# The second MLP's first layer by seven products of halves in place of eight, with its gates split in the last layer

## The chip, the cores and the metric

The kernel runs on one core of a Trainium2 chip. The metric is the time of one execution in microseconds (us) on the device. The engines are named as the profile names them: PE (TensorE matmul), PEld (its weight load), DVE (VectorE), ACT (ScalarE), POOL (GpSimd) and SP (the engine that issues the transfers). Matrices lie in SBUF with 128 partitions; matmul results go to PSUM, which has eight banks of 512 float32 columns.

## The reference

A causal attention feeds two MLPs in a row; all inputs are float32.

```python
attn_out = _attn_ref(q, k, v)                 # 2 batches x 12 heads x 448 x 64, causal softmax
x = attn_out.transpose(0, 2, 1, 3).reshape(896, 768)

def _moe_ref(x, w_gate, w_val, w_out):        # 768 -> 1536 -> 768
    g = x @ w_gate
    silu = g * (1.0 / (1.0 + np.exp(-g)))
    val = x @ w_val
    return silu * val @ w_out

def _moe2_ref(x, w_in, w_out):                # 768 -> 2048 -> 768
    h = x @ w_in
    relu6 = np.clip(h + 3.0, 0.0, 6.0)
    g = h * relu6 / 6.0
    return g @ w_out
```

## The kernel before

**Products in three.** The weights arrive as 64-bit floats. Each MLP product is made from two float32r parts of each operand, a high part (the operand rounded) and a low part (the rest): `mm3_parts` (L183) issues high x high, high x low and low x high into one PSUM bank. So each term of a product is three matmuls of a 128 x 128 weight tile with 384 or 512 token columns (`PARTS`; 896 tokens together).

**Weights.** `w_unit` makes one unit of 768 x 128 weights (or 256 x 384 in the last layer): a DMA to `raw`, an unpacking on ACT (L112), a shift and an OR on DVE (L117, L118; the OR reads `raw` and `w`, both in SBUF), the high part on ACT (`whi`, L121), the low part on POOL (`wlo`, L122; it reads `w` and `whi`). The units run in a ring of four `whi`/`wlo` slots, three `raw` and two `w` buffers, two units ahead of their use; the cast to a slot waits until PE has done the slot's old unit. Each engine works through its own queue in order.

**Stages.** Attention comes first. The gate and value layers of the first MLP follow (24 units, 864 matmuls, results to `g1`), then w_out (12 units, 432 matmuls, results to `x2`), then the second MLP's first layer (16 units, one per block f of 128 hidden features, 576 matmuls), then the last layer in two column halves (L566, 672 matmuls of 384 columns: the gates are the weight tiles, the weights the moving operand). For a block f, both token parts are gated: a clipped ramp on ACT (L554), its product with the result on DVE (L555), then `split` makes the gates' high part on ACT (L165) and their low part on DVE (L166). The last layer reads these parts in both column halves.

**Order.** A scheduler merges the code into one queue for each engine; `high_priority` (`SOON`) puts the work on results ahead. The last layer keeps its last two weight units (`LATE`) for an end in which the token tiles finish one after the other.

## Time and profile before

| | |
|---|---|
| median of 3 runs | 616.59 us (616.4 to 617.06) |
| profiled execution | 616.48 us, span 614.7 us |
| PE busy | 608.2 us (99%), 3617 matmuls |
| DVE, ACT, POOL busy | 280.5, 265.4, 183.4 us |
| DMA | 70.15 MB, mean 114 GB/s |

Start with the share of PE and the chain that ended last. The mean duration of a matmul is longer than the distance between two, because they overlap; distances are read from the timeline. The means of ACT, DVE and POOL are durations of one instruction from its start to its end; two independent ones behind each other overlap by some 0.09 us.

### The profile page before, as it was taken

Reading aid. Unit: us, or ns where it says so; the run is one execution under the profiler, and the core shown is the slowest. Engines: PE = TensorE matmul, PEld = TensorE weight load, DVE = VectorE, ACT = ScalarE, POOL = GpSimd, SP = SyncE. Lnnn points to the kernel's source line nnn. Section 1 sums busy time; section 2 is a strip of 40 time slices with the busy share of each in tenths; the row PEclk is TensorE's granted clock in tenths of the full one; section 3 lists DMA queues with packets and bytes.
Section 4 is the critical chain, followed back from the end, with each engine's and each line's share of the span. In section 5 each row is a group of like instructions: output and inputs, shape, how many; then the busy total and the mean of one; then the engine's idle time right before and its main releaser. Section 6 shows DMA issues by size and latency. Waiting matters only on the chain.

```text
span 614.7 us, 9332 instructions
## 1 busy us (share of the span) xinstructions
PE 608.2 (99%) x3617; PEld 561.9 (91%) x3618; DVE 280.5 (46%) x622; ACT 265.4 (43%) x452; POOL 183.4 (30%) x126
## 2 busy tenths in 40 slices
PE   8999999999999999999999999999999999999997
PEld 5999999889999888889999888889998899999997
DVE  6888888675433344334322333454544542123001
ACT  5687777745433333333323223555545532223100
POOL 4555653233222222222222222222222222213200
PEclk9999999999999999999999999999999999999999
DMA  9555545356433333333333333333433333452002
GB/s 181 133 131 128 137 113 157 111 189 213 151 107 104 103 102 103 103 114 124 121 104 102 103 103 102 104 109 115 129 110 103 102 103 103 107 177 65 0 1 91
DMA packets 83917, 70.15 MB, mean 114 GB/s; under 512 B 35232, under 2 KB 79776, under 8 KB 83872
## 3 DMA queue, kind: packets, MB, share of 16 engines
q1 hardware_dynamic: 83872, 69.55, 39.2%
q8 instruction: 29, 0.48, 0.3%
q14 instruction: 16, 0.13, 0.1%
HBM read 61.73 MB, written 2.75 MB: 105 GB/s over the span
## 4 chain that ended last, share of the span: by engine, by line
PE 97%; DVE 1%; ACT 1%; issue 0%; POOL 0%; DVEq 0%; ACTq 0%
PE mm L183 61%; PE mm L566 19%; PE pv L414 6%; PE sc L343 5%; PE tp L386 4%; PE tr L268 1%; PE zero L207 1%; PE tr L448 1%; DVE e L356 0%; DVE qq L281 0%; PE tr L298 0%; POOL wlo L122 0%; ACT e L366 0%; ACT w L112 0%; DVE qq L314 0%
## 5 line engine op out<-in xcount | busy, mean ns | idle before, releaser
L122 POOL TENSOR_TENSOR wlo<-w,whi 128x768 fp32r<-128x768 f32 (+1 forms) x69 | 126.1, 1828 | 356.7 <-ACT whi L121 299.7
L117 DVE TENSOR_SCALAR w<-w 128x768 uint32<-128x768 uint32 (+1 forms) x69 | 39.9, 578 | 191.1 <-ACT w L112 191.0
L121 ACT CAST whi<-w 128x768 fp32r<-128x768 f32 (+1 forms) x69 | 57.0, 826 | 127.7 <-PE mm L183 85.4
L183 PE MATMUL mm<-x1h,wlo 128*128 128x384 f32 (+1 forms) x288 | 105.0, 365 | 0.4 <-POOL wlo L122 0.4
L183 PE MATMUL mm<-x1l,whi 128*128 128x384 f32 (+1 forms) x288 | 104.7, 364 | 0.0
L183 PE MATMUL mm<-x1h,whi 128*128 128x384 f32 (+1 forms) x288 | 104.6, 363 | 0.0
L112 ACT ACTIVATE w<-raw 128x768 f32<-128x768 f32 (+1 forms) x69 | 61.1, 887 | 95.8 <-POOL wlo L122 95.3
L566 PE MATMUL mm<-whi,gl 128*128 128x384 f32 x224 | 74.8, 334 | 0.0
L566 PE MATMUL mm<-whi,gh 128*128 128x384 f32 x224 | 74.8, 334 | 0.0
L566 PE MATMUL mm<-wlo,gh 128*128 128x384 f32 x224 | 74.8, 334 | 0.0
L414 PE MATMUL pv<-v,et 112*112 112x65 f32 x480 | 73.4, 242 | 0.0
L183 PE MATMUL mm<-x2h,wlo 128*128 128x384 f32 (+1 forms) x192 | 69.9, 364 | 0.0
L118 DVE SCALAR_TENSOR_TENSOR w<-raw,w 128x768 uint32<-128x768 uint32 (+1 forms) x69 | 69.1, 1002 | 1.7
L183 PE MATMUL mm<-x2l,whi 128*128 128x384 f32 (+1 forms) x192 | 69.8, 364 | 0.0
L183 PE MATMUL mm<-x2h,whi 128*128 128x384 f32 (+1 forms) x192 | 69.6, 362 | 0.0
L414 PEld LDWEIGHTS pv<-v,et 112*112 112x112 f32 x480 | 65.6, 177 | 1.2
L386 PE MATMUL tp<-ident,e 112*112 112x112 f32 x240 | 61.2, 260 | 1.2 <-ACT e L366 1.2
L183 PEld LDWEIGHTS mm<-x1h,whi 128*128 128x128 f32 x288 | 54.1, 188 | 6.4 <-ACT whi L121 0.4
L183 PEld LDWEIGHTS mm<-x1h,wlo 128*128 128x128 f32 x288 | 54.0, 188 | 6.3 <-POOL wlo L122 0.6
L183 PEld LDWEIGHTS mm<-x1l,whi 128*128 128x128 f32 x288 | 54.1, 188 | 6.1
L366 ACT ACTIVATE e<-e,m 112x336 f32<-112x336 f32 (+1 forms) x96 | 48.7, 530 | 19.9 <-DVE m L356 19.9
L165 ACT CAST gh<-mm 128x384 fp32r<-128x384 f32 (+1 forms) x56 | 29.6, 529 | 53.3 <-DVE mm L520 26.4
(71 smaller groups left out, 1019.5 us busy)
## 6 DMA issues: line engine op xcount, KB each, us to landing
raw<-in_moe_w_out_dram SPq DMA_DIRECT2D x28, 768.0 KB, 4.3
raw<-in_moe_w_in_dram SPq DMA_DIRECT2D x16, 768.0 KB, 4.6
raw<-in_moe_w_gate_dram SPq DMA_DIRECT2D x12, 768.0 KB, 4.2
raw<-in_moe_w_val_dram SPq DMA_DIRECT2D x12, 768.0 KB, 4.3
kn<-in_k_dram SPq DMA_DIRECT2D x24, 112.0 KB, 2.7
qn<-in_q_dram SPq DMA_DIRECT2D x24, 112.0 KB, 2.7
v<-in_v_dram SPq DMA_DIRECT2D x12, 224.0 KB, 3.2
out_dram<-ob SPq DMA_DIRECT2D x14, 192.0 KB, 1.8
```

The source lines that it names most:

```text
L112: first = nc.scalar.activation(out=w[:, p], in_=high.bitcast(F32), func=AF.Prelu, scale=2.0**-112, alpha=2.0**32)
L117: nc.vector.tensor_scalar(out=wu, in0=wu, scalar1=3, scalar2=None, op0=ALU.logical_shift_left)
L118: nc.vector.scalar_tensor_tensor(out=wu, in0=low, scalar=29, in1=wu, op0=ALU.logical_shift_right, op1=ALU.bitwise_or)
L121: nc.scalar.copy(hi[:, p], w[:, p])
L122: nc.gpsimd.tensor_tensor(out=lo[:, p], in0=w[:, p], in1=hi[:, p].bitcast(F32), op=ALU.subtract)
L165: nc.scalar.copy(hi, src)
L183: lambda lhs=lhs, rhs=rhs, i=i: nc.tensor.matmul(ps, lhs, rhs, start=(first and i == 0), stop=(last and i == total - 1))
L343: nc.tensor.matmul(sp[:C, o : o + w], t["qq"][:, j, c * C : (c + 1) * C], t[("kk", "k2")[i]][:, j, 0:w], start=(i == 0), stop=(i == 1),)
L366: nc.scalar.activation(out=es, in_=es, func=AF.Exp, scale=-1.0, bias=m[:, x : x + 1])
L386: nc.tensor.transpose(tp[:C, at - lo : at - lo + C], e[:, at : at + C], ident[:C, :C])
L414: nc.tensor.matmul(box["o"][:, qc, :], et[:, at : at + C], vt[:, j, c, :], start=(c == 0), stop=(c == qc))
L566: nc.tensor.matmul(acc, lhs[:, tsl], rhs[:, i, :], start=(fc == 0 and n == 0), stop=(fc == K2 - 1 and n == 2),)
```

## The change

**Seven products.** Blocks are taken in pairs j (f = 2j and 2j + 1). The 768 input features are cut in halves of 384, the tokens in the two batches of 448, the pair's features in its two blocks: a product of 2 x 2 by 2 x 2 blocks, which eight half products would make, is made from seven and sums (Winograd's form of Strassen's scheme). A half product is 3 terms x 3 = 9 matmuls of 448 columns. The code names them p1 to p7, and `seven` spells out which weight operand meets which x operand; the names below are used further on.

- x operands, made once in w_out's loop from its results: B11, B21, B22 and the sums T1, T2, T3, T4. They lie in one tile `xmem`, in whose first part `x1` lies too. T2 = B22 - B12 + B11 is complete only with the last of w_out's columns.
- weight operands of a pair: w(j) = A11 and A12, s(j) = S1 and S2, v(j) = S3 and A22, d(j) = S4, each as high and low parts, in a ring of five slots (four for a pair). `pair_units` unpacks the pair's two units and makes the sums: two half-sums of 384 on DVE (L565, L566), two differences of 384 on POOL (L569, L570). `pair_rest` splits v and d.
- PE's order: p1(j), p4(j-1), p6(j), p3(j-1), p7(j), p2(j), p5(j). p6 needs s(j), p7 needs v(j), p1 needs w(j).
- results: a copy u0 of p1 on ACT, seven sums on DVE (L668), which make u1, u2 and the four blocks a, b, c, d in PSUM; each block is gated (L637, L639). p4 writes into the bank that the sum for u2 reads, p3 into the one that b's sum and the second u1 read.

**Gates in float32.** Fifteen blocks of gates stay float32 (`g2`); the last layer splits a block three blocks ahead of its use, in each column half anew (`g_split`: a cast of 896 on ACT, L764, and a difference of 896 on DVE, L765), into the space of `xmem` in the order in which the x operands fall free. Block 0 is split at once.

**Buffers.** Two `raw`, three `w`, three weight slots until w_out is done, five behind it. w_out takes its columns in the order 0, 3, 1, 4, 2, 5 and in token halves of 448.

```diff
-    for e in range(KD):
+    E_ORDER = [e for i in range(KD // 2) for e in (i, i + KD // 2)]
+    for e in E_ORDER:
...
+        def pair_units(j):
+            ws = [ring.tile([128, KD, 128], F32, tag="w", name="w", bufs=3) for _ in range(2)]
+            for n in range(2):
+                for step in w_unit(cols(w2_in, 2 * j + n), KD, 128, w=ws[n]):
+                    step()
+            w, v = ws
+            s = ring.tile([128, KD, 128], F32, tag="s", name="s", bufs=1)
+            parts = {"w": w_parts(KD, 128)}
+            w_split(*parts["w"], w)
+            nc.vector.tensor_tensor(out=s[:, :KH], in0=v[:, :KH], in1=v[:, KH:], op=ALU.add)
+            nc.vector.tensor_tensor(out=s[:, KH:], in0=s[:, :KH], in1=w[:, :KH], op=ALU.subtract)
+            parts["s"] = w_parts(KD, 128)
+            w_split(*parts["s"], s)
+            nc.gpsimd.tensor_tensor(out=v[:, :KH], in0=w[:, :KH], in1=v[:, :KH], op=ALU.subtract)
+            nc.gpsimd.tensor_tensor(out=w[:, KH:], in0=w[:, KH:], in1=s[:, KH:], op=ALU.subtract)
+            return w, v, parts
+
+        def pair_rest(w, v, parts):
+            parts["v"] = w_parts(KD, 128)
+            w_split(*parts["v"], v)
+            parts["d"] = w_parts(KD, 128)
+            w_split(*(t[:, KH:] for t in parts["d"]), w[:, KH:])
...
-        for e in range(KD):
+        for n, e in enumerate(E_ORDER):
+            if n == KD - 1:
+                first_pair = pair_units(0)
...
+                    t1, b11, n11 = held.pop(i)
+                    t2 = side(512, "t2")[:, :S]
+                    lo21 = keep("B21", i, pts[0])
+                    nc.vector.tensor_tensor(out=t2, in0=pts[1], in1=t1, op=ALU.subtract)
+                    rest(nc.vector, *lo21)
+                    rest(nc.gpsimd, *keep("T2", i, t2))
+                    nc.vector.tensor_tensor(out=b11, in0=t2, in1=b11, op=ALU.subtract)
+                    rest(nc.vector, *keep("T3", i, b11))
+                    nc.vector.tensor_tensor(out=pts[0], in0=pts[0], in1=t2, op=ALU.subtract)
+                    rest(nc.vector, *keep("T4", i, pts[0]))
+                    rest(nc.vector, *keep("B22", i, pts[1]))
...
+        cycle[:] = [cycle[0], cycle[1], WB, WB + 1, cycle[2]]
...
+            g = pt if f == 0 else g2[f - 1][:, bs]
+            nc.vector.scalar_tensor_tensor(out=g, in0=sg, scalar=1.0, in1=pt, op0=ALU.min, op1=ALU.mult)
...
+            def p1():
+                product("a", "A11", "B11")
+                soon(lambda: nc.scalar.copy(u0, at["a"]))
+
+            def p6():
+                product("b", "S2", "T2")
+                soon(lambda: add(u1, at["b"], u0))
+
+            def p7():
+                product("d", "S3", "T3")
+                soon(lambda: add(u2, at["d"], u1))
+
+            def p2():
+                product("a", "A12", "B21")
+
+                def end():
+                    add(at["a"], at["a"], u0)
+                    done("a", f, 0)
+
+                soon(end)
+
+            def p5():
+                product("c", "S1", "T1")
+
+                def end():
+                    add(at["b"], at["c"], u2)
+                    add(u1, at["c"], u1)
+                    done("b", f + 1, 1)
+
+                soon(end)
+
+            def p4():
+                product("d", "A22", "T4")
+
+                def end():
+                    add(at["d"], at["d"], u2)
+                    done("d", f + 1, 0)
+
+                soon(end)
+
+            def p3():
+                product("c", "S4", "B22")
+
+                def end():
+                    add(at["c"], at["c"], u1)
+                    done("c", f, 1)
+
+                soon(end)
+
+            return [p1, p6, p7, p2, p5], [p4, p3]
...
+            nc.scalar.copy(hi, g2[fc - 1])
+            nc.vector.tensor_tensor(out=lo, in0=g2[fc - 1], in1=hi.bitcast(F32), op=ALU.subtract)
```

**POOL's queue where w_out ends.** Before, the rows are one low part for each unit; these five are w_out's last three units and the first two of w2_in.

```order
L122 TENSOR_TENSOR wlo1_3589<-w_3587,whi1_3588 128x768
L122 TENSOR_TENSOR wlo2_3641<-w_3639,whi2_3640 128x768
L122 TENSOR_TENSOR wlo3_3687<-w_3685,whi3_3686 128x768
L122 TENSOR_TENSOR wlo0_3739<-w_3737,whi0_3738 128x768
L122 TENSOR_TENSOR wlo1_3785<-w_3783,whi1_3784 128x768
```

With the change (w_3757, s_3769, w_3758 are w, s, v of pair 0, w_3900 is w of pair 1; t1 and t2 are x sums, T1 and T2):

```order
L100 TENSOR_TENSOR wlo2_3707<-w_3705,whi2_3706 128x768
L100 TENSOR_TENSOR wlo0_3771<-w_3757,whi0_3770 128x768
L553 TENSOR_TENSOR xmem_71<-t1_3750,xmem_71 128x448
L570 TENSOR_TENSOR w_3757<-w_3757,s_3769 128x384
L100 TENSOR_TENSOR wlo1_3777<-s_3769,whi1_3776 128x768
L100 TENSOR_TENSOR wlo2_3893<-w_3758,whi2_3892 128x768
L100 TENSOR_TENSOR wlo3_3914<-w_3900,whi3_3913 128x768
L553 TENSOR_TENSOR xmem_71<-t2_3856,xmem_71 128x448
```

T2's last low part, which the second product of pair 0 needs, has come to stand behind two weight units.

**DVE's queue in the middle of the layer.** Before, twelve rows are two blocks (the last of the layer; the rows of the others are the same):

```order
L118 SCALAR_TENSOR_TENSOR w_4801<-raw0_4800,w_4801 128x768
L555 SCALAR_TENSOR_TENSOR mm_1_4625<-r6_4644,mm_1_4625 128x384
L166 TENSOR_TENSOR gl13_4624<-mm_1_4625,gh13_4623 128x384
L555 SCALAR_TENSOR_TENSOR mm_6_4649<-r6_4668,mm_6_4649 128x512
L117 TENSOR_SCALAR w_4853<-w_4853 128x768
L166 TENSOR_TENSOR gl13_4624<-mm_6_4649,gh13_4623 128x512
L118 SCALAR_TENSOR_TENSOR w_4853<-raw1_4852,w_4853 128x768
L555 SCALAR_TENSOR_TENSOR mm_5_4685<-r6_4704,mm_5_4685 128x384
L166 TENSOR_TENSOR gl14_4684<-mm_5_4685,gh14_4683 128x384
L555 SCALAR_TENSOR_TENSOR mm_3_4709<-r6_4728,mm_3_4709 128x512
L117 TENSOR_SCALAR w_4905<-w_4905 128x768
L166 TENSOR_TENSOR gl14_4684<-mm_3_4709,gh14_4683 128x512
```

With the change, the first twelve rows of a round (w_4494 is v of pair 6, s_4505 its half-sums, w_4616 the w of pair 7, d_1_4454 and c_6_4478 are blocks of pair 4, b_3_4545 and u1_4519 belong to pair 5):

```order
L126 TENSOR_SCALAR w_4494<-w_4494 128x768
L127 SCALAR_TENSOR_TENSOR w_4494<-raw_4500,w_4494 128x768
L668 TENSOR_TENSOR d_1_4454<-d_1_4454,u2_4397 128x448
L565 TENSOR_TENSOR s_4505<-w_4494 128x384
L566 TENSOR_TENSOR s_4505<-s_4505,w_4493 128x384
L126 TENSOR_SCALAR w_4616<-w_4616 128x768
L639 SCALAR_TENSOR_TENSOR g2_9_3883<-r6_4542,d_1_4454 128x448
L668 TENSOR_TENSOR u1_4519<-b_3_4545,u0_4518 128x448
L127 SCALAR_TENSOR_TENSOR w_4616<-raw_4618,w_4616 128x768
L668 TENSOR_TENSOR c_6_4478<-c_6_4478,u1_4396 128x448
L668 TENSOR_TENSOR u2_4520<-d_2_4577,u1_4519 128x448
L639 SCALAR_TENSOR_TENSOR g2_8_3882<-r6_4566,c_6_4478 128x448
```

POOL's rows for the same round (w_4493 is w of pair 6):

```order
L100 TENSOR_TENSOR wlo2_4447<-w_4371,whi2_4446 128x768
L100 TENSOR_TENSOR wlo0_4451<-w_4370,whi0_4450 128x384
L569 TENSOR_TENSOR w_4494<-w_4493,w_4494 128x384
L100 TENSOR_TENSOR wlo3_4507<-w_4493,whi3_4506 128x768
L570 TENSOR_TENSOR w_4493<-w_4493,s_4505 128x384
L100 TENSOR_TENSOR wlo4_4513<-s_4505,whi4_4512 128x768
```

ACT's rows there (u0 is p1's copy, r6 the ramps of the gates):

```order
L121 ACTIVATE w_4494<-raw_4500 128x768
L676 COPY u0_4518<-a_5_4521 128x448
L99 CAST whi0_4450<-w_4370 128x384
L121 ACTIVATE w_4616<-raw_4618 128x768
L637 ACTIVATE r6_4542<-d_1_4454,half_58 128x448
L99 CAST whi3_4506<-w_4493 128x768
L637 ACTIVATE r6_4566<-c_6_4478,half_58 128x448
L99 CAST whi4_4512<-s_4505 128x768
```

Per pair, DVE has seven sums and two half-sums more and no low parts of gates; POOL has four instructions more than two. The cast of s and the sum that it comes behind stand after the OR of the next pair's w.

**DVE's queue at the end of the layer.** Before, the last gates are followed by weight units alone:

```order
L555 SCALAR_TENSOR_TENSOR mm_2_4745<-r6_4764,mm_2_4745 128x384
L166 TENSOR_TENSOR gl15_4744<-mm_2_4745,gh15_4743 128x384
L555 SCALAR_TENSOR_TENSOR mm_7_4769<-r6_4788,mm_7_4769 128x512
L117 TENSOR_SCALAR w_4957<-w_4957 128x768
L166 TENSOR_TENSOR gl15_4744<-mm_7_4769,gh15_4743 128x512
L118 SCALAR_TENSOR_TENSOR w_4957<-raw0_4956,w_4957 128x768
```

With the change (u1_4750 and u2_4751 belong to the last pair; w_4883 is the third unit of the last layer; g2_2, g2_3, g2_4 are float32 gates):

```order
L126 TENSOR_SCALAR w_4883<-w_4883 128x768
L765 TENSOR_TENSOR xmem_71<-g2_2_3876,xmem_71 128x896
L668 TENSOR_TENSOR c_6_4724<-c_6_4724,u1_4642 128x448
L127 SCALAR_TENSOR_TENSOR w_4883<-raw_4882,w_4883 128x768
L668 TENSOR_TENSOR u2_4751<-d_2_4800,u1_4750 128x448
L639 SCALAR_TENSOR_TENSOR g2_12_3886<-r6_4797,c_6_4724 128x448
L765 TENSOR_TENSOR xmem_71<-g2_3_3877,xmem_71 128x896
L668 TENSOR_TENSOR a_5_4752<-a_5_4752,u0_4749 128x448
L765 TENSOR_TENSOR xmem_71<-g2_4_3878,xmem_71 128x896
L668 TENSOR_TENSOR b_3_4776<-c_7_4824,u2_4751 128x448
L639 SCALAR_TENSOR_TENSOR g2_14_3888<-r6_4821,a_5_4752 128x448
L668 TENSOR_TENSOR u1_4750<-c_7_4824,u1_4750 128x448
```

The last layer's splits have moved in between the sums of the last pair. On PE five matmuls of the last layer stand between the last p4 and the last p3.

## Rows read from the trace of the kernel before

**Rows 1.** The page's busy times: engine, busy us (share of the span), instructions.

```profile
PE 608.2 (99%) x3617; PEld 561.9 (91%) x3618; DVE 280.5 (46%) x622; ACT 265.4 (43%) x452; POOL 183.4 (30%) x126
```

**Rows 2.** The chain that ended last, its last long stretches: start, us, engine, line.

```profile
118.69 376.00 PE mm L183 x1860
494.69 116.52 PE mm L566 x672
```

**Rows 3.** Windows: stretch, length, busy us (instructions) of PE, PEld, DVE, ACT, POOL, clock, DMA.

```profile
379.00:494.70 115.70, 115.70 (x574) 103.81 (x573) 59.59 (x95) 58.93 (x96) 29.43 (x16) 1.00 0.37 107
```

**Rows 4.** Timeline of PE, 18 rows of 384 columns, then 512: start, us.

```profile
400.06 0.33 PE L183 MATMUL mm<-x2h,whi 128*128 128x384 f32 x1
...
403.21 0.39 PE L183 MATMUL mm<-x2h,whi 128*128 128x512 f32 x1
...
405.97 0.39 PE L183 MATMUL mm<-x2h,whi 128*128 128x512 f32 x1
```

**Rows 5.** Groups by line and form, DVE: busy us, mean ns, idle before.

```profile
L118 DVE SCALAR_TENSOR_TENSOR w<-raw,w 128x768 uint32<-128x768 uint32 x67 | 68.0, 1015 | 1.7
L117 DVE TENSOR_SCALAR w<-w 128x768 uint32<-128x768 uint32 x67 | 39.2, 585 | 191.0 <-ACT w L112 191.0
L555 DVE SCALAR_TENSOR_TENSOR mm<-r,mm 128x512 f32<-128x512 f32 x16 | 11.2, 697 | 21.8 <-ACT r L554 21.8
L555 DVE SCALAR_TENSOR_TENSOR mm<-r,mm 128x384 f32<-128x384 f32 x16 | 8.9, 555 | 0.0
L118 DVE SCALAR_TENSOR_TENSOR w<-raw,w 128x384 uint32<-128x384 uint32 x2 | 1.1, 558 | 0.0
```

**Rows 6.** Groups by line and form, ACT.

```profile
L112 ACT ACTIVATE w<-raw 128x768 f32<-128x768 f32 x67 | 60.0, 897 | 95.8 <-POOL wlo L122 95.3 <-DMA raw<-in_moe_w_val_dram 0.5
L121 ACT CAST whi<-w 128x768 fp32r<-128x768 f32 x67 | 56.0, 836 | 127.7 <-PE mm L183 85.4 <-PE mm L566 37.9 <-DVE w L118 4.4
L554 ACT ACTIVATE r<-mm,half 128x512 f32<-128x512 f32 x16 | 10.9, 682 | 0.0
L554 ACT ACTIVATE r<-mm,half 128x384 f32<-128x384 f32 x16 | 9.4, 590 | 0.0
L121 ACT CAST whi<-w 128x384 fp32r<-128x384 f32 x2 | 1.0, 510 | 0.0
```

**Rows 7.** Groups by line and form, POOL.

```profile
L122 POOL TENSOR_TENSOR wlo<-w,whi 128x768 fp32r<-128x768 f32 x67 | 123.8, 1849 | 342.5 <-ACT whi L121 285.5 <-DVE mm L520 48.8 <-issue 8.2
L122 POOL TENSOR_TENSOR wlo<-w,whi 128x384 fp32r<-128x384 f32 x2 | 2.3, 1142 | 14.2 <-ACT whi L121 14.2
```

**Rows 8.** Timeline of DVE around the first units, and in the changed layer.

```profile
117.23 0.55 DVE L117 TENSOR_SCALAR w<-w 128x768 uint32<-128x768 uint32 x1
117.81 1.64 DVE L118 SCALAR_TENSOR_TENSOR w<-raw,w 128x768 uint32<-128x768 uint32 x1
...
123.53 0.96 DVE L118 SCALAR_TENSOR_TENSOR w<-raw,w 128x768 uint32<-128x768 uint32 x1
...
132.33 2.63 DVE L118 SCALAR_TENSOR_TENSOR w<-raw,w 128x768 uint32<-128x768 uint32 x1
...
411.07 0.56 DVE L117 TENSOR_SCALAR w<-w 128x768 uint32<-128x768 uint32 x1 [1.61 <-ACT w L112]
```

**Rows 9.** Timeline of POOL in the same stretches.

```profile
114.54 1.00 POOL L122 TENSOR_TENSOR wlo<-w,whi 128x384 fp32r<-128x384 f32 x1 [12.39 <-ACT whi L121]
117.36 1.28 POOL L122 TENSOR_TENSOR wlo<-w,whi 128x384 fp32r<-128x384 f32 x1 [1.81 <-ACT whi L121]
...
132.29 1.85 POOL L122 TENSOR_TENSOR wlo<-w,whi 128x768 fp32r<-128x768 f32 x1 [4.93 <-ACT whi L121]
...
408.27 1.84 POOL L122 TENSOR_TENSOR wlo<-w,whi 128x768 fp32r<-128x768 f32 x1 [5.12 <-ACT whi L121]
```

**Rows 10.** Timeline of ACT in the changed layer.

```profile
407.30 0.83 ACT L121 CAST whi<-w 128x768 fp32r<-128x768 f32 x1 [0.17 <-PE mm L183]
...
410.14 0.89 ACT L112 ACTIVATE w<-raw 128x768 f32<-128x768 f32 x1 [1.42 <-POOL wlo L122]
```

More of the change, by code (lines that the diff above doesn't have):

```diff
@@ L137, in tile_attention_glu_mlp @@
             units.append((cols(rows, e), KD, 128))
-    for f in range(K2):
-        units.append((cols(w2_in, f), KD, 128))
+    NU = len(units)
     for eh in range(2):
@@ L150, in prefetch @@
     def prefetch(n):
-        while len(made) < min(n, len(units)):
+        while len(made) < min(n, last_unit[0]):
             for step in w_unit(*units[len(made)]):
@@ new lines, in mlps, with gates @@
+        early.close()
+        more.append(ctx.enter_context(tc.tile_pool(name="more", bufs=1)))
+        cycle[:] = [cycle[0], cycle[1], WB, WB + 1, cycle[2]]
+        nc.vector.memset(half, 0.5)
+        g2 = [more[0].tile([128, NT], F32, name=f"g2_{f}") for f in range(1, K2)]
+        g2_parts = [more[0].tile([128, NT], F32R, name=f"g2_0{p}") for p in "hl"]
+        def gates(pt, f, b):
+            bs = slice(b * S, (b + 1) * S)
+            sg = side(512, "r6")[:, :S]
+            nc.scalar.activation(out=sg, in_=pt, func=AF.Relu, scale=1.0 / 6.0, bias=half[:, 0:1])
+            g = pt if f == 0 else g2[f - 1][:, bs]
+            nc.vector.scalar_tensor_tensor(out=g, in0=sg, scalar=1.0, in1=pt, op0=ALU.min, op1=ALU.mult)
+            if f == 0:
+                split(*[t[:, bs] for t in g2_parts], pt)
@@ new lines, in seven, with product, soon, add @@
+        def seven(j, ops):
+            f = 2 * j
+            at, use = {}, {}
+            def product(nm, a, b):
+                if nm not in at:
+                    t, use[nm] = bank(nm)
+                    at[nm] = t[:, :S]
+                (wh, wl), h = ops[a]
+                bh, bl = x2[b]
+                mm3(
+                    at[nm],
+                    [(wh[:, h * KH + i], wl[:, h * KH + i], bh[:, i], bl[:, i]) for i in range(KH)],
+                )
+            def soon(fn):
+                with tc.high_priority(offset=SOON):
+                    fn()
+            u0 = more[0].tile([128, S], F32, tag="u0", name="u0", bufs=1)
+            u1 = more[0].tile([128, S], F32, tag="u1", name="u1", bufs=2)
+            u2 = more[0].tile([128, S], F32, tag="u2", name="u2", bufs=2)
+            def add(out, ps, u):
+                nc.vector.tensor_tensor(out=out, in0=ps, in1=u, op=ALU.add)
+            def done(nm, block, b):
+                gates(at[nm], block, b)
+                idle.append(use[nm])
+            def p1():
[33 more added lines that the diff above has]
+            return [p1, p6, p7, p2, p5], [p4, p3]
@@ new lines, in mlps @@
+        NPAIR2 = K2 // 2
+        after = []
+        ops = pair_rest(*first_pair)
+        for j in range(NPAIR2):
+            if j + 1 < NPAIR2:
+                ahead = pair_units(j + 1)
+            else:
+                last_unit[0] = len(units)
+                prefetch(NU + 1)
+            now, later = seven(j, ops)
+            now[0]()
+            if after:
+                after[0]()
+            now[1]()
+            if after:
+                after[1]()
+            if j + 1 < NPAIR2:
+                ops = pair_rest(*ahead)
+            for fn in now[2:]:
+                fn()
+            after = later
@@ L559, in mlps @@
+        g_parts0 = g2_parts
         TT = NT // 128
```

125 lines of the change are left out of this document (83 added, 42 removed).

## The prediction

> **What bounds the kernel now.** I read the page's head first: PE is busy for 608.2 us, 99% of the span [rows 1]. The chain of waits then shows where that is the end's cause: behind 118.69 us the chain is nothing but two stretches of matmuls, 376.00 us for the layers up to and with the changed one and 116.52 us for the last layer [rows 2]. The windows by stage show the changed layer alone: 115.70 us, PE busy in all of it, DVE for 59.59, ACT 58.93, POOL 29.43 [rows 3]. So PE is the bound there, and what counts is how fast matmuls follow each other. The duration of one (0.33 to 0.40 us) is no measure of that, since they overlap: 18 of 384 columns start in 3.15 us (0.175 each), 12 of 512 in 2.76 us (0.230 each) [rows 4]. By the code L183 has 864 + 432 + 576 = 1872 matmuls; 376.00 / 1872 = 0.2009 us, the mean of both widths. No f32r matmul of 448 columns on 128 x 128 is in the trace; its price lies between 0.175 and 0.230, and midway, so I take 0.2009. The profiled execution took 616.48 us, 0.1 under the median of 616.59; I sum against 616.48.
>
> **What PE saves.** The layer has 576 matmuls now and 8 pairs x 7 products x 9 = 504 then: 72 x 0.2009 = 14.5 us. A product is 1.81 us, a pair 12.66 instead of 14.46. The w_out layer and the last layer keep their counts and columns. With all else hidden: 616.5 - 14.5 = 602.0 us.
>
> **What the others get, per pair.** Now, by the window: DVE 59.59 / 8 = 7.4 us, ACT 7.4, POOL 3.7 [rows 3]. Then DVE has two shifts and two ORs (0.585 and 1.015), four gate products and seven sums of PSUM with SBUF (0.626 each, the mean of L555's forms), two half-sums of 384 (0.558, by the OR of 384) [rows 5]: 11.2 us. ACT has two unpackings (0.897), three casts (0.836), a half cast (0.510), four gates (0.636) and a PSUM copy (about 0.56, between the casts of 384 and 768): 7.9 us [rows 6]. POOL has three low parts of 1.849 and three instructions of 384 (1.142) [rows 7]: 9.0 us. Each is below 12.66, so by busy time alone the gain would stand.
>
> **What the busy time hides.** DVE's OR of 768 takes 0.96 us; at 132.33 one took 2.63 and at 117.81 one took 1.64 [rows 8], and in both a POOL low part was running, 132.29 to 134.14 and 117.36 to 118.64 [rows 9]: the OR ended 0.82 us after POOL did. So an OR (two SBUF sources) stands still while POOL works. The reverse shows too: POOL's 384 took 1.28 us where DVE's shift was still running when it began, 1.00 elsewhere [rows 8, 9]. Now these meet twice in 69, because ACT's unpacking waits for POOL's low part (0.03 us behind its end) and DVE's shift for the unpacking (0.04) [rows 8 to 10]. In a pair of the new layer POOL has 8.5 us of work (3 x 1.84 + 3 x 1.00) and DVE 4.2 us of shifts, ORs and half-sums that must lie between: 12.7 us, as long as PE's pair, if they packed without a gap. They don't.
>
> For the half-sums, and for the splits of 896 in the last layer (L765), no row shows whether POOL holds them. Bounds: not held, or held as the OR is. I take held, the row being the nearest (DVE, two SBUF sources). The Trainium skill (SBUF — State Buffer, "Who interferes with whom") says of any DVE instruction with two SBUF inputs that a GpSimd instruction which reads SBUF blocks it for its whole length. By that rule the sum is the one below, 618.8; by the two OR rows alone it would be 1.1 us less, 617.7, all of it at the layer's end (split g4 below).
>
> **A round.** I followed the queues' order with these durations (POOL starts 0.1 behind a cast, DVE and ACT 0.03 behind what they wait for [rows 8 to 10]), from the end of POOL's low part of s(j), for rounds in which these three, and not PE, are late. POOL v low part to 1.87. ACT: unpack v(j+1), whose tile that frees, to 2.80; copy u0 to 3.22; cast d(j) to 3.64. DVE: shift to 3.39, OR to 4.39. POOL d low part is ready at 3.74, held by the OR to 4.39, done 5.25. DVE's first half-sum is held to 5.25, done 5.67, the second 6.27. ACT: unpack w(j+2) to 6.18, gate to 6.73, cast w(j+1) to 7.47. POOL: v difference to 7.13, w low part 7.57 to 9.41. DVE: shift to 7.55, gate product, u1, then the OR for w(j+2), ready at 8.54, held to 9.41, done 10.23; behind it in DVE's queue the sum for c, 10.77. ACT: gate of c to 11.44 and, queued behind it, the cast of s(j+1) to 12.18. POOL: s low part 12.28 to 14.12. A round is 14.1 us, not 12.66: 0.35 under the old pair. Without the holds the same walk gives 12.2. If POOL's next instruction beats a waiting OR at 9.41, it gives 15.0. Half-sums held or not change nothing here, since the cast of w(j+1) sets 7.57.
>
> **The start.** At the last w_out matmul (zero) POOL has v(0), w(1) and only then T2's last low part in its queue: casts end at 0.73 and 1.47, POOL at 2.67, 4.54 and about 5.75. The second product has run seven of nine matmuls by 3.2: PE idles 2.5 us. In that slack the next pair is made: s(2)'s low part ends at 28.2 while PE wants it at 28.3. So no wait until then; the next round, still with the first gate's splits and a late v(2), is 14.9, and s(3) is there at 43.0.
>
> **The end.** Four rounds on, s(7) is there at 43.0 + 4 x 14.1 = 99.4. PE then needs 1.4 us for that product and six more, 10.85: 111.7 if nothing came between. But the gate splits of the last layer now stand in ACT's and DVE's queues (0.97 and 1.12 us each: 768's rows x 896/768) between the sums. DVE: split g1 to 3.0, shift, sum, OR to 5.2, gate product, u1 6.2, shift 7.5, split g2 8.5, sum 9.0, OR held by POOL's low part of the first w2_out unit to 10.5, 11.3, u2 11.9. PE's next-to-last product waits for u2: from 8.6 to 11.9. Then gate product, split g3 13.4, sum, split g4 held to 15.1, 16.1, sum, gate product, u1 17.7; PE's last product waits for that: from 14.5 to 17.7. Together 6.4 us.
>
> **Sum.** 99.4 + 12.2 + 6.4 = 118.0 us for the layer against 115.7: **618.8 us**, 0.4% slower. In the last layer a pass over two blocks is 42 x 0.1734 = 7.3 us (116.52 / 672 [rows 2]); ACT gets about 3.7 there, DVE's shift, OR and two splits 3.8 beside POOL's 1.85: hidden. So are, in w_out (28.9 us per two columns), five more instructions on DVE, four on ACT and two on POOL; that cover gone would cost what the start costs. The third raw buffer and fourth weight slot, taken from the first layers, cost nothing: a cast may start when PE leaves a unit (7.2 us), 2.9 us later the unit is whole, and it is wanted two units on.
>
> **Rivals.** (A) The above. Its own range: 615 (rounds of 13.6, end 1.5 shorter) to 622 (rounds of 15.0). (B), the other side: the holds hardly bite, because PE's pace puts POOL's and DVE's instructions beside each other less often than my walk. For it: busy times of 11.2, 7.9 and 9.0 all fit 12.66, and the walk without holds gives 12.2. Against: two held ORs, and POOL at 9 of 12.66 us leaves few free places. Then the layer is 101.3 + 2.5 and about 2 at the end: 105.8, so 606.6 us. It decides from rounds under 13.5: 43.0 + 4 x 13.5 + 18.6 = 115.6, the old layer. (C) The holds stack up: the ties go to POOL, and a late u1 or u2 stops PE in each round as at the end. For it: four gates in each round go DVE, ACT, DVE in a fixed order. Against: in the walk u1 and u2 have 0.6 us and more to spare. Rounds of 15.0 and an end of 8: 43.5 + 4 x 15.0 + 12.2 + 8 = 123.7, so 624.5 us. (D) Idle PE lowers its granted clock. No row shows a fall: the clock is 1.00, the level of 2.4 GHz, in the window [rows 3], and PE never idles there. At half the clock, 2 us of matmuls in each round would cost 2 more: 8 x 2 + 618.8 = 635.
>
> **Chances.** A 0.48, B 0.30, C 0.18, D 0.04. About 0.2% is what a measurement here can tell from no change: 615.4 to 617.8 is "same". A puts 0.29 above that, 0.14 in it, 0.05 below; B lies below, C and D above, but for 0.02 of each of B and C that reach "same". Faster 0.33, same 0.18, slower 0.49. The range takes in B's and C's middles: 606 to 625.
>
> **What would show it.** Windows of one round (seven products) in the middle of the layer: about 14 us, PE busy 90%; PE's waits on the third matmul of the S2 product, released by POOL's low part (L100); OR (L127) means well over 1 us, up to 2.7; half-sums over 0.6. At the layer's start one wait of 2.5 us on L553's low part on POOL; at its end two of about 3 us, released by L668. Wrong if: ORs stay near 1 us or rounds near 12.7 (B); PE waits on L668 in every round (C); the granted clock under 1 (D); or a new idle stretch in w_out or the last layer.

## The result and the profile after

The changed kernel takes 623.71 us (median of 4 runs, 620.74 to 624.2), the kernel before 616.82 beside it: ratio 1.0102, 95% interval 1.007 to 1.0135. It is slower by 1.0%. The profiled execution took 623.45 us.

The page's busy times answer to [rows 1]:

```profile
PE 603.2 (97%) x3545; PEld 556.9 (90%) x3546; DVE 362.0 (58%) x709; ACT 295.4 (48%) x488; POOL 244.4 (39%) x164
```

PE has its 72 matmuls less, but only 5 us less busy time, and 3% of the span idle where it was 1%. The windows say where (stretch, length, busy us and instructions of PE, PEld, DVE, ACT, POOL, granted clock, DMA): the whole layer, two rounds in its middle, and two short stretches behind its long waits.

```profile
379.30:502.20 122.90, 111.32 (x511) 96.81 (x510) 103.31 (x145) 69.93 (x105) 77.78 (x48) 0.97 0.35 103
437.85:451.97 14.12, 13.57 (x65) 11.60 (x63) 11.83 (x17) 7.23 (x13) 10.00 (x7) 1.00 0.38 113
451.97:466.07 14.10, 13.57 (x65) 11.60 (x63) 11.83 (x17) 7.23 (x13) 9.99 (x7) 1.00 0.39 111
385.00:389.50 4.50, 4.49 (x14) 4.03 (x15) 2.85 (x5) 0.00 (x0) 0.00 (x0) 0.62 0.08 16
498.60:502.20 3.60, 3.52 (x10) 3.17 (x11) 2.55 (x5) 3.52 (x5) 0.10 (x1) 0.53 0.01 2
```

The layer takes 122.9 us; five of the last layer's matmuls (0.9 us) lie in it, so 122.0 against 115.7 [rows 3]. A round, from one S2 product's start to the next, takes 14.1 us from 437.85 on; the three rounds ahead of that took 13.0, 15.2 and 13.3 (S2 products at 396.34, 409.36 and 424.51). In the last two stretches the clock is 0.62 and 0.53 in the mean, so most of them ran at 1.2 GHz, and neither has a wait of any length. PE's waits in the layer (who waited for whom: us in total, times, longest):

```profile
PE d L194 <- DVE u L668: 3.9, 6, 2.9
PE c L194 <- DVE u L668: 3.1, 2, 2.8
PE b L194 <- POOL xmem L553: 2.3, 1, 2.3
PE b L194 <- POOL wlo L100: 1.2, 4, 0.3
PE a L194 <- POOL wlo L100: 1.1, 1, 1.1
```

Three long waits stand out, one at the start (L553) and two at the end (the sums of L668); the 1.1 us on L100 stand in the fourth pair's p1, in the round of 15.2. The timeline of PE gives their places and what lies behind them (start, us, instruction, and in brackets the idle time before it):

```profile
385.01 0.47 PE L194 MATMUL b<-xmem,whi 128*128 128x448 f32 x1 [2.30 <-POOL xmem L553]
385.52 0.57 PE L194 MATMUL d<-xmem,whi 128*128 128x448 f32 x2
...
388.45 0.95 PE L194 MATMUL a<-xmem,whi 128*128 128x448 f32 x2
...
447.54 0.57 PE L194 MATMUL a<-xmem,whi 128*128 128x448 f32 x2
...
450.04 0.68 PE L194 MATMUL d<-xmem,whi 128*128 128x448 f32 x2 [0.20 <-DVE u L668]
...
451.97 0.57 PE L194 MATMUL b<-xmem,whi 128*128 128x448 f32 x2
452.83 0.47 PE L194 MATMUL b<-xmem,wlo 128*128 128x448 f32 x1 [0.29 <-POOL wlo L100]
...
461.65 0.57 PE L194 MATMUL a<-xmem,whi 128*128 128x448 f32 x2
462.27 0.47 PE L194 MATMUL a<-xmem,wlo 128*128 128x448 f32 x1
...
464.15 0.66 PE L194 MATMUL d<-xmem,whi 128*128 128x448 f32 x2 [0.19 <-DVE u L668]
...
492.90 0.67 PE L194 MATMUL d<-xmem,whi 128*128 128x448 f32 x2 [2.88 <-DVE u L668]
494.82 0.34 PE L777 MATMUL mm<-whi,g_0h 128*128 128x384 f32 x1
498.68 1.12 PE L194 MATMUL c<-xmem,whi 128*128 128x448 f32 x2 [2.80 <-DVE u L668]
...
502.16 0.33 PE L777 MATMUL mm<-whi,g_0l 128*128 128x384 f32 x1
```

A product of nine matmuls that nothing stops takes 1.82 us from start to start (1.86 in some stretches). Behind the first wait the S3 product took 2.93 (385.52 to 388.45), behind the last one the S4 product 3.48 (498.68 to 502.16). Distances also show what the idle times of a round hide. The rows show two waits, 0.20 behind p1 and 0.29 in the S2 product, and p1 took 2.50 us, because the end of the matmul before is modelled late. A third wait shows no idle time at all: p1's third matmul starts at 462.27, 0.62 us behind the first where 0.41 is usual, just behind the end of POOL's low part of w (462.21, in the rows below). Seven products that nothing stops take 12.77 us (run 11 below), so the three small waits, 0.49 by these rows, cost 14.1 - 12.77 = 1.3 us.

The timeline of POOL in one round:

```profile
450.93 1.85 POOL L100 TENSOR_TENSOR wlo<-s,whi 128x768 fp32r<-128x768 f32 x1 [1.14 <-ACT whi L99]
...
456.60 1.50 POOL L100 TENSOR_TENSOR wlo<-w,whi 128x384 fp32r<-128x384 f32 x1 [1.89 <-issue]
458.65 1.33 POOL L569 TENSOR_TENSOR w<-w 128x384 f32<-128x384 f32 x1 [0.56 <-DVE s L565]
460.36 1.85 POOL L100 TENSOR_TENSOR wlo<-w,whi 128x768 fp32r<-128x768 f32 x1 [0.38 <-ACT whi L99]
...
465.04 1.85 POOL L100 TENSOR_TENSOR wlo<-s,whi 128x768 fp32r<-128x768 f32 x1 [1.13 <-ACT whi L99]
```

And of DVE in the same round:

```profile
456.26 0.96 DVE L127 SCALAR_TENSOR_TENSOR w<-raw,w 128x768 uint32<-128x768 uint32 x1
...
457.67 0.84 DVE L565 TENSOR_TENSOR s<-w 128x384 f32<-128x384 f32 x1
458.54 0.56 DVE L566 TENSOR_TENSOR s<-s,w 128x384 f32<-128x384 f32 x1
459.06 1.33 DVE L126 TENSOR_SCALAR w<-w 128x768 uint32<-128x768 uint32 x1
...
461.38 1.64 DVE L127 SCALAR_TENSOR_TENSOR w<-raw,w 128x768 uint32<-128x768 uint32 x1
462.95 0.62 DVE L668 TENSOR_TENSOR c<-c,u 128x448 f32<-128x448 f32 x1
463.49 0.61 DVE L668 TENSOR_TENSOR u<-d,u 128x448 f32<-128x448 f32 x1
```

The half-sum that began at 457.67, the shift at 459.06 and the OR at 461.38 each ended 0.4 to 0.8 us after the POOL instruction that was running. The sum for u2 stands behind that OR and ends at 464.10; PE's p4 starts at 464.15.

At the layer's end, the timeline of POOL:

```profile
489.68 1.81 POOL L100 TENSOR_TENSOR wlo<-w,whi 128x768 fp32r<-128x768 f32 x1 [2.56 <-DVE xmem L765]
494.13 1.94 POOL L100 TENSOR_TENSOR wlo<-w,whi 128x768 fp32r<-128x768 f32 x1 [2.64 <-ACT whi L99]
```

And of DVE, the OR ahead of the last u2 and the split ahead of the last u1:

```profile
490.09 2.22 DVE L127 SCALAR_TENSOR_TENSOR w<-raw,w 128x768 uint32<-128x768 uint32 x1
494.83 2.20 DVE L765 TENSOR_TENSOR xmem<-g,xmem 128x896 fp32r<-128x896 f32 x1
```

### The profile page after: what moved, and what is told of

Read it like the earlier page. It is cut to its first block, busy times and chain, and to the rows that moved or that the text cites. A ratio compares the mean times of both kernels' runs of the same rounds, so it can differ in the third digit from the quotient of the medians.

```text
span 621.4 us, 9384 instructions
## 1 busy us (share of the span) xinstructions
PE 603.2 (97%) x3545; PEld 556.9 (90%) x3546; DVE 362.0 (58%) x709; ACT 295.4 (48%) x488; POOL 244.4 (39%) x164
## 5 line engine op out<-in xcount | busy, mean ns | idle before, releaser
L100 POOL TENSOR_TENSOR wlo<-w,whi 128x768 fp32r<-128x768 f32 (+1 forms) x77 | 144.2, 1874 | 272.4 <-ACT whi L99 191.0
L194 PE MATMUL mm<-xmem,whi 128*128 128x384 f32 (+1 forms) x576 | 163.0, 363 | 0.0
L194 PEld LDWEIGHTS mm<-xmem,whi 128*128 128x128 f32 x576 | 106.2, 188 | 12.4 <-ACT whi L99 0.4
L777 PE MATMUL mm<-whi,xmem 128*128 128x384 f32 x420 | 107.0, 334 | 0.0
L194 PE MATMUL mm<-xmem,wlo 128*128 128x384 f32 (+1 forms) x288 | 105.0, 365 | 0.4 <-POOL wlo L100 0.4
L777 PEld LDWEIGHTS mm<-whi,xmem 128*128 128x128 f32 x420 | 75.9, 188 | 0.0
L777 PE MATMUL mm<-wlo,xmem 128*128 128x384 f32 x210 | 70.1, 334 | 0.0
L194 PEld LDWEIGHTS mm<-xmem,wlo 128*128 128x128 f32 x288 | 54.0, 188 | 6.3 <-POOL wlo L100 0.6
L194 PE MATMUL mm<-gh,whi 128*128 128x448 f32 x144 | 52.6, 365 | 0.0
L194 PE MATMUL mm<-gl,whi 128*128 128x448 f32 x144 | 52.6, 365 | 0.0
L194 PE MATMUL mm<-gh,wlo 128*128 128x448 f32 x144 | 52.6, 365 | 0.0
L765 DVE TENSOR_TENSOR xmem<-g,xmem 128x896 fp32r<-128x896 f32 x30 | 37.5, 1267 | 7.4 <-ACT xmem L764 7.4
```

Source lines behind the costliest of these rows:

```text
L100: nc.gpsimd.tensor_tensor(out=lo, in0=w, in1=hi.bitcast(F32), op=ALU.subtract)
L194: lambda lhs=lhs, rhs=rhs, i=i: nc.tensor.matmul(ps, lhs, rhs, start=(first and i == 0), stop=(last and i == total - 1))
L765: nc.vector.tensor_tensor(out=lo, in0=g2[fc - 1], in1=hi.bitcast(F32), op=ALU.subtract)
L777: nc.tensor.matmul(acc, lhs[:, tsl], rhs[:, i, :], start=(fc == 0 and n == 0), stop=(fc == K2 - 1 and n == 2),)
```

## The experiments

All times are medians; "before" ran beside them, at 616.5 to 616.8 us. Line numbers of quoted rows are those of the experiment's own kernel.

### 1. The splits behind the last sums

```diff
 for g in range(NG - LATE):
-    w = next_unit()
-    ... g_split(...)
+    with tc.issue_after(last_u1[0].ins):   # the second u1 of pair 7, on DVE
+        w = next_unit()
+        ... g_split(...)
```

> The low parts of the gate splits (L765), and the shift and OR of the second and later units of the last layer, stand in DVE's queue behind the last pair's two sums with the last c product; nothing else is changed. Theory (the two waits at the layer's end, 2.88 and 2.80 us, come from splits and an OR queued ahead of the sums, and each wait is followed by matmuls at half the granted clock): both waits are gone, -5.7 us, -0.3 for two restarts of the matmul pipeline, -1.8 for the 9 matmuls of the last product that took 3.6 us: 615.9 us; if the last layer then waits for a split or a unit that comes later, up to 618. Rival 1 (the half clock is no consequence of the waits): -5.7 to -6.0 alone, 617.9, with a granted clock below 1 still there at the layer's end. Rival 2 (not the splits but the held OR makes the sums late): the first wait stays, about 620.5.

Measured: 624.77 us, ratio 1.0131 (1.0117 to 1.0145): no gain. The layer is shorter: the end waits are 0.90 and 1.54 (the theory had them gone), and it takes 115.5 us, 6.5 less; 1.6 of that is the start, where the same wait was followed by the full clock in this profile. But PE then waits in the last layer (the view of PE's waits again):

```profile
PE mm L779 <- DVE ob L811: 3.9, 1, 3.9
PE mm L779 <- DVE xmem L767: 0.7, 1, 0.7
```

The later splits, 1.1 to 2.7 us each, left DVE late: the first output copy (L811) at the change of column halves came 54.3 us behind the last layer's sixth matmul (495.08 to 549.37), where run 2 takes 46.7 (496.74 to 543.41). PE waited there for a bank (until 560.14), and the window behind it (560 to 565) has a clock of 0.66. The wait was not removed but moved some 70 us on. The theory had allowed up to 2 us for the last layer; it took back all 6.5.

### 2. T2's last low part on DVE

```diff
-rest(nc.gpsimd, *keep("T2", i, t2))
+rest(nc.vector if i == KH - 1 else nc.gpsimd, *keep("T2", i, t2))
```

> The third low part of T2 (L553), for which PE waits 2.30 us in the first S2 product, goes to DVE, one instruction of 0.62 us ahead of the other low parts; nothing else moves in any queue. Theory (the whole layer follows PE's start, since the weight slots come free only as PE leaves them): the wait goes (-2.3), the pipeline restart (-0.2), and the 3 us of matmuls at half the clock behind it (-1.6): 619.6 us. Rival (from the second pair on the weights' making sets the pace and had run ahead in that pause): the first rounds wait for what the start no longer does, 622.5 us or more. Rival 2 (the half clock is not the wait's doing): -2.5, 621.2, with a granted clock near 0.84 still there behind the start.

Measured: 617.95 us, ratio 1.0027 (1.0018 to 1.0036), 5.8 us under the changed kernel. The wait is gone, the clock is 1.00 from 378 to 480, and the rounds begin earlier by as much: the layer follows its start. The matmuls from the first S2 product to the first p5 take 3.9 us less (380.60 to 386.31, where the changed kernel has 381.13 to 390.76). Another 1.5 us come from the end. PE's timeline there:

```profile
489.04 0.67 PE L194 MATMUL d<-xmem,whi 128*128 128x448 f32 x2 [2.75 <-DVE u L668]
...
492.01 0.52 PE L777 MATMUL mm<-whi,g_0h 128*128 128x384 f32 x1
...
494.81 0.67 PE L194 MATMUL c<-xmem,whi 128*128 128x448 f32 x2 [1.25 <-DVE u L668]
...
496.74 0.34 PE L777 MATMUL mm<-whi,g_0l 128*128 128x384 f32 x1
```

Here the half clock fell behind the first end wait: p4 took 2.97 us in place of 1.92. That cost nothing, for the last product had to wait for its sum in any case: it starts 5.77 us behind p4's start, as before (5.78), with 1.25 us of wait in place of 2.80. The last product itself ran at the full clock, 1.93 us in place of 3.48, and this is the gain. That the stretch fell where a wait covered it was luck: nothing was changed at the end.

### 3. The long waits filled with matmuls

```diff
 def p6():
+    if j == 0: fill(11, "A11", "B11")      # matmuls into a spare bank
 def p4():
+    if j == NPAIR2 - 1: fill(14, "S1", "T1")
 def p3():
+    if j == NPAIR2 - 1: fill(14, "A22", "T4")
```

> The long waits of PE are filled with 448-column matmuls whose result nobody reads: 11 ahead of the first S2 product, 14 ahead of each of the last two products (0.20 us each). DVE, ACT and POOL do the same work, but the scheduler places a few of their instructions differently. Theory (an idle PE of 2.3 us and more is what lowers the granted clock): the granted clock is 1.00 in every stretch of the layer, and the time falls by what the half clock cost, 1.6 us at the start and 1.8 at the end: 620.3 us. Rival (the slow matmuls behind a wait have another cause, their operands or the sequencer's restart): the slow stretches stay, 623.7 us, or more by fillers that outlast the waits, up to 625.

Measured: 625.85 us, ratio 1.015 (1.0136 to 1.0164): slower, against the expectation, and inconclusive as a measure of the price. Within the layer the theory held: the clock is 1.00 in all windows to 500, and the layer 1.2 us shorter. But the fillers displaced the five matmuls that the last layer had put into the wait, and there PE waited 1.81 us for a gate (L639), with a clock of 0.84 from 505 to 515 behind it.

### 4. The OR with one SBUF source

```diff
-scalar_tensor_tensor(out=wu, in0=low, scalar=29, in1=wu, shift_right, or)
+tensor_scalar(out=wu, in0=low, scalar1=29, op0=shift_right)
```

> In the second MLP's two layers the OR of 768 (raw and w, two SBUF sources) becomes a shift of raw alone (one strided SBUF source): the weights' upper bits are left out, so the product is not the reference's. Count of instructions and what waits for what stay. Theory (ORs that stand still beside POOL's low parts stretch the round from the 12.2 us of the walk to 14.1): no instruction of this line lasts past 1.0 us, rounds of about 13 us (PE's own seven products are 12.8), seven rounds 1.0 shorter: 616.5 us. Rival (load, not holds: 9 us of POOL with what it waits for fill the round): the rounds stay at 13.9 or more, 622 us. In between if half-sums and shifts are held alike: rounds of 13.5, 619.

Measured: 622.03 us, ratio 1.0084 (1.0071 to 1.0098). Rounds of 13.7 us (wait to wait 446.01, 459.69, 473.38): between the theories; the time is the rival's. It was no clean test: alone the instruction lasts 0.56 us, as the shift does, and it was still held (mean 0.77), and so were half-sums (0.96 for the second, mean). The order on DVE and POOL changed in every round as well.

### 5. Start mended, three splits kept early

The second run, and the first with `issue_after` for the first pass (g = 0) alone.

> T2's third low part on DVE, as in the run before, and at the layer's end only the first three gate splits and the first unit of the last layer behind the last pair's sum for the last product, so that the other splits keep their early places. Theory (the layer loses at its two seams about 11.6 us, waits with the slow matmuls behind them, and the late splits alone gave the gain of the first run back): no wait at either seam over 0.7 us but the one of 0.7 us in the second pair, layer of 112.5 us, no wait in the last layer: 612.0 us. Rival (the last layer has no room for splits that come later, however few): the seam is mended and 2 to 6 us come back as waits in the last layer, 614 to 618.

Measured: 621.92 us, ratio 1.0091 (1.0075 to 1.0106): the rival, and worse. The first sum's wait at the end is down to 0.73 us, but two of the three splits stand between it and the second u1, and the last product waited 2.1 us: 114.3 us for the layer (378.68 to 493.52, without 0.5 for three matmuls of the last layer). Then waits of 1.6 us (a split, L767) and 2.1 us (an output copy) came in the last layer, with clocks of 0.87 and 0.79 from 555 to 565.

### 6. A fourth w buffer

```diff
-w = ring.tile(..., tag="w", bufs=3)
+w = w_tile(a, b)      # three tags in ring, a fourth in the freed gate memory
```

> A fourth buffer for the unpacked weights w, in the freed gate memory, so that ACT's unpacking no longer waits for POOL's low part of two units before; the scheduler moves some instructions of the first rounds with it. Theory 1 (in the round the engines wait for each other's queues: POOL for a cast on ACT that is queued behind an unpacking that waits for POOL): the round falls from 14.1 us to PE's own 12.8, the layer by seven times 1.2: 615.5 us. Theory 2 (POOL's and DVE's two-source instructions exclude each other and fill the round): the round stays at 13.6 or more, 621 us or slower.

Measured: 621.36 us, ratio 1.0074 (1.0062 to 1.0087). From the third to the eighth S2 product (413.15 to 482.56) five rounds took 13.9 us in the mean (12.8 to 15.0): theory 2. The order on DVE and POOL changed in these rounds too, so the run shows that this buffer does not bring PE's pace, and no more. With the unpacking free, the holds went to other instructions; a half-sum took 2.05 us. POOL's timeline:

```profile
468.58 1.85 POOL L109 TENSOR_TENSOR wlo<-w,whi 128x768 fp32r<-128x768 f32 x1
```

DVE's, with the half-sum (L574 there) ending 0.42 us after it:

```profile
468.80 2.05 DVE L574 TENSOR_TENSOR s<-w 128x384 f32<-128x384 f32 x1
```

### 7. The half differences on DVE

```diff
-nc.gpsimd.tensor_tensor(out=v[:, :KH], ...)
-nc.gpsimd.tensor_tensor(out=w[:, KH:], ...)
+nc.vector.tensor_tensor(...)   # both
```

> The two half differences of a pair (L569, L570) go from POOL to DVE: 2.0 to 2.6 us less on POOL in a round, 1.1 us more on DVE (two SBUF sources each, 0.56 us unheld). Theory 1 (the wait of the queues for each other): POOL is shorter by the v difference in the loop, rounds of 13.2 to 13.6, 618 us. Theory 2 (exclusion): POOL's 6.5 us and DVE's 5.3 us of two-source work are 11.8 where they were 12.7, rounds of 13.0, 616. Rival 3 (DVE becomes the bound: 12.3 us of its own and in-order waits): rounds of 14.1 or more, 623.5 us and slower.

Measured: 629.32 us, ratio 1.0207 (1.0184 to 1.0229): rival 3, and by more than it said. The last three rounds took 16.2 us, DVE busy for 14.1 of them; a difference took 1.93 us beside a low part. So less work on POOL does not help when the work goes to the queue that holds the sums.

### 8. No second SBUF source

```diff
-in1=wu                      # OR
+in1=<one column of zeros in PSUM, broadcast>
-in1=v[:, KH:]  ;  in0=s[:, :KH], in1=w[:, :KH]      # half-sums
+in1=<the same>  ;  in0=w[:, :KH], in1=<the same>
```

> In the new layer and the w_out layer before it the ORs and the two half-sums read, in place of their second SBUF source, one column of zeros in PSUM: same instructions, same order in every queue, same waits, only the source differs (the weights lose their upper bits and the half-sums one half, so the product is not the reference's). Theory 1 (a DVE instruction with two SBUF sources and POOL's work exclude each other, and that stretches the round): ORs near 1.0 us and half-sums near 0.6 throughout, rounds of PE's 12.8 us or little more (13.2), the layer 6 to 9 us shorter: 615 to 617.5. Theory 2 (each engine's queue waits for the others' in a ring, whatever the ports do): ORs short as well, but rounds of 13.7 or more: 621 and more.

Measured: 614.07 us, ratio 0.9956 (0.9943 to 0.997), 9.6 us under the changed kernel, with the same instructions (and one memset). POOL's and PE's order is the same throughout, that of DVE and ACT but for a few instructions that changed places in the first rounds (those that the changed kernel starts before 418 us). Two rounds in the window view (columns as for the changed kernel):

```profile
434.89:447.91 13.02, 13.02 (x64) 11.83 (x63) 10.64 (x18) 7.46 (x12) 8.84 (x7) 1.00 0.40 121
447.91:460.93 13.02, 13.02 (x64) 11.83 (x63) 10.62 (x18) 7.36 (x12) 8.82 (x7) 1.00 0.43 122
```

PE has no wait in any round, and its products set the pace (here 1.86 us each). The ORs took 0.95 us in the mean, DVE's busy time fell from 11.83 to 10.6. Theory 1: the second SBUF source alone makes the difference between 14.1 and 13.0. From the second to the eighth S2 product this run needs 78.1 us where the changed kernel needs 83.9, and the first wait at the end, behind the OR that was held there, fell from 2.88 to 1.02. The shift in SBUF was still held (1.2 us beside L572, POOL's first half difference in this kernel).

### 9 and 10. The first splits on POOL, and with the fourth buffer

```diff
-nc.vector.tensor_tensor(out=lo, in0=g2[fc - 1], ...)
+eng = nc.gpsimd if 1 <= n < 6 else nc.vector
```

on top of run 5; run 10 adds run 6's buffer.

> T2's third low part on DVE, the last pair's sums ahead of the first splits and of the second unit of the last layer on DVE, and the low parts of the first five gate splits on POOL (about 2.2 us each, by 1.85 for 768 columns), which has 13 us with little to do at that seam. Rounds are untouched. Theory (the end seam is short of DVE time, not of POOL time): waits of 0.7 us at most at the layer's end, none in the last layer, 5.1 us under the run with T2's low part on DVE alone (2.1 and 1.3 of waits, 0.3 of restarts, 1.5 of slow matmuls): 612.8 us, faster than the kernel before. Rival (POOL's five splits hold up the ORs and delay the second unit): waits of 2 us and more in the last layer, 616 and more.

> The kernel of the run before with the fourth w buffer. Theory (rounds of 13.9 us in place of 14.1, as that buffer gave alone, seams as in the run before): 1.4 us less than the run before, 611.4 us. Rival (that buffer's reordering of the first rounds costs what the later rounds give, since it showed waits of 1.9 and 1.2 us there that the start's wait partly hid): 613 to 615, no better than without it.

Measured: 617.14 us, ratio 1.0006 (0.9997 to 1.0015), and 616.76 us, ratio 1.0007 (0.9996 to 1.0018): no different from before. Both miss their theories, 612.8 and 611.4. In run 9 the layer is 114.0 us long and the last layer has one wait of 1.4 us; but the last product still waited 1.84 us, because one split (L768, 1.33 us, held by POOL) still stood on DVE ahead of the last sums. The layer's end was not freed of what it was meant to be freed of. In run 10 the waits of 0.5 and 1.9 us that the fourth buffer had shown in the first rounds (run 6) came back as 0.8 and 1.9, and in its profile the clock behind the second is 0.50 (400 to 404).

### 11 and 12. The OR's second source in PSUM

```diff
-w unpacked, shifted and ORed in SBUF
+ps = top_pool.tile([128, 2, 512], F32)      # two spare PSUM banks
+nc.scalar.activation(out=ps, in_=high, ...)
+nc.vector.tensor_scalar(out=ps, in0=ps, scalar1=3, shift_left)
+nc.vector.scalar_tensor_tensor(out=wu, in0=low, scalar=29, in1=ps, shift_right, or)
```

on top of run 9; run 12 does it for the first weight of a pair alone.

> The kernel with the first splits on POOL, and from the second pair on both weights of a pair are unpacked by ACT into two spare PSUM banks (one buffer, six banks left for products), shifted there by DVE, and the OR reads raw from SBUF and w from PSUM and writes w to SBUF: it computes what the reference does, and no OR of the layer has two SBUF sources. The price is the shift, which in PSUM will take about as long as the OR (0.95 us in place of 0.56): 0.8 us more DVE per pair, 12.0 in all. Theory (the exclusion of DVE's two-source instructions and POOL stretches the round): ORs of 1.0 us, rounds of 13.3 us, the layer 5 us shorter: 612 us, faster than the kernel before. Rival (DVE at 12.0 of 13 us with its in-order waits sets the round, as the two half differences on DVE did): rounds of 14.1 or more, 617 us and slower.

> As the run before, but only the first weight of a pair goes through PSUM: in the rounds of the changed kernel it is its OR that meets POOL's low part and lasts 1.64 us, while the other's takes 0.96. DVE's price is 0.4 us in a pair. Theory (exclusion): rounds of 13.4 to 13.6 us, 614 us. Rival (the hold only moves to the next two-source instruction, a half-sum or the other OR): rounds of 14.0, 617 us.

Measured: 617.14 us, ratio 1.0008 (0.9999 to 1.0017), and 620.47 us, ratio 1.006 (1.0047 to 1.0074). In run 11 the mechanism is there from the fifth pair on (windows of two rounds):

```profile
453.46:466.23 12.77, 12.77 (x65) 11.84 (x63) 11.74 (x19) 7.31 (x11) 8.00 (x7) 1.00 0.56 170
466.23:479.00 12.77, 12.77 (x64) 11.84 (x63) 10.78 (x17) 6.73 (x10) 9.69 (x7) 1.00 0.43 124
```

Rounds at PE's own pace, DVE at 11.7 and 10.8 us of 12.8, no wait: the time is the rival's, the late rounds are better than the theory's. From there to the last S2 product it needs 38.3 us (440.70 to 479.00) where run 9 needs 42.3 (434.26 to 476.53). But up to there it needs 60.4 us (from 380.27) where run 9 needs 53.3: the single PSUM buffer makes the first pairs' weights late (at 405.77 ACT's unpacking had waited 3.04 us for an OR to free it), and PE waits for low parts (L100 is L108 there):

```profile
PE b L213 <- POOL wlo L108: 4.0, 3, 2.3
PE d L213 <- POOL wlo L108: 1.7, 2, 1.0
```

So the gain of the late rounds went into the early ones. Run 12 has the early waits too (47.4 us to the fourth S2 product, 380.28 to 427.71, where run 9 needs 40.1), and then rounds of 13.0 to 13.9, 13.3 in the mean: the theory's, and a little better, but the time missed both forecasts. A kernel with run 11's late rounds and run 9's early ones would be some 4 us faster than run 9 by these sums; it was not run, and no kernel here that does the whole work beats the kernel before.

## Why the prediction was right, and what was missing in it

The forecast was 618.8 us and slower (0.49), with a range of 606 to 625. The time is 623.71, slower, near the upper end. It lies outside the 615 to 622 that the forecast gave its own account (A). Step by step:

**What PE saves.** 72 x 0.2009 = 14.5 us was right in kind: undisturbed, nine matmuls take 1.82 us (1.81 forecast) or, in some stretches, 1.86.

**The holds and the round.** Forecast: ORs that stand still beside POOL, a round of 14.1 us against 12.2 without the holds. Measured: 14.10 to 14.13 in the three rounds from 437.85. The walk fits not only by its sum. Counted from 452.78, where POOL's low part of s ends, the first half-sum ends at 5.73 us (walk: 5.67), POOL's v difference at 7.20 (7.13), the shift at 7.61 (7.55), the OR at 10.24 (10.23), the sum for c at 10.79 (10.77) and the next low part of s at 14.11 (14.12). That the holds are the cause is shown by run 8: the same queues without the second SBUF source run at PE's pace; in run 6 a fourth buffer alone does not bring that pace. Half-sums and splits are held as the ORs are: half-sums of 0.84 and 2.05 us, a split of 2.20 us (from 494.83, POOL's low part 494.13 to 496.07). The Trainium skill (SBUF — State Buffer, "Who interferes with whom") says so of all DVE instructions with two SBUF inputs, and these rows agree. The shift is held too: 1.33 us beside L569, where the busy-time sum has 0.585. The walk has it held as well, from 6.27 to 7.55, 0.42 us behind the end of POOL's v difference. In PSUM (run 11) it took 0.95 us, also beside POOL's work. The Trainium skill (SBUF — State Buffer, "Who interferes with whom") says that DVE instructions in a two-port mode take the ports that it shares with GpSimd as well, and names `tensor_scalar`, the shift's form, among those that can; the rows agree.

**PE at 90% in a round** was wrong as a sign: the window says 96%, because matmuls' ends are modelled; 13.57 of 14.1 us "busy" hold 12.77 us of work (run 11's round). The distances between starts show it.

**The start.** A wait of 2.5 us for T2's last low part: 2.30. Run 2 shows the place and the cause right.

**The end.** Waits of 3.3 and 3.2 us for the sums behind a held OR and a held split: 2.88 and 2.80 of idle, 3.0 each by the distances. The OR ended 0.82 us after POOL's low part, the split 0.96.

**The step that was missing: what follows a long wait.** The sum, 99.4 + 12.2 + 6.4 = 118.0, has no term for the clock; rival D saw it as a matter of the rounds, at 16 us, and got 0.04. The rounds' short waits left the clock at 1.00. Two of the three long waits did not: 1.6 us lost behind the first (2.93 and 2.31 us for products of 1.82) and 1.7 behind the last (3.48); behind the one of 2.88 nothing was lost (492.90 to 494.82). Of the 4.0 us by which the layer exceeds the forecast, 3.3 are these; the rest, 0.7, is of the size of 56 products at 1.82 to 1.86 us where 1.81 was taken. (Another 0.7 of the profiled execution's time lies outside the layer.) Run 1's profile prices the start: it has the same wait at the full clock, and its last S2 product starts 99.2 us behind the layer's first matmul, the changed kernel's 100.9. Run 2 takes away the first wait, and the start falls by 3.9 us, not by 2.5; the rest of its 5.8 us is mostly the luck at the end.

**Where 14.5 us went.** 56 products at 1.825 are 102.2 us, 13.5 under the old layer. Six rounds (396.34 to 480.20, 83.86 us) lost 7.2 against 76.65; the start 2.5 and 1.6; the end 6.0 and 1.7. That makes 121.2 of the 122.0; the small wait in the last S2 product and products of 1.86 are the rest. Each of the three parts alone is less than the saving; together they are 19.0 us.

**Rivals.** B fell with the rounds, 14.1 where it needed under 13.5. C's sign came: PE waits for u2 in five rounds (0.20 each), behind the held OR, so u2 did not have the 0.6 us to spare that the walk gave it. C's sizes did not: the rounds are as long as the walk without that wait had them, not 15.0, and the end lost 6.0 us in waits, not 8. D's sign came too, a clock of 0.97 in the layer, but behind the long waits and not in the rounds. So 623.71 is beside C's 624.5 by luck, through the clock. The stated range held because it reached up to C's middle; A's sum alone was 4.9 us short.

## What to carry to other kernels

When a change gives a busy engine less to do and its helpers more, ask not only for their busy time but for which of their instructions cannot run beside each other; here 11.2 us of DVE's and 9.0 us of POOL's work fitted a round of 12.8 by sum, and needed 14.1 because much of it excluded each other. Look at the seams of the pipeline as well: the start and the end cost 11.8 us, more than the holds of six rounds, and mending one seam by delaying work moved the wait to the next place where that work was short of cover. Price a wait of the matmul engine by the distance between starts, and, if it is long, by the matmuls behind it too.
